# Maxima of the feature map in PSUM, constants on GpSimd, omega's parts read from PSUM, and half of one expert's second low parts on VectorE

## The chip, the cores and the metric

The program runs on one core of one Trainium2 chip. A core has TensorE for matrix products, VectorE and ScalarE for element work (both reach SBUF and PSUM), GpSimd for element work in SBUF, and DMA queues. The metric is the device time of one execution in microseconds; lower is better.

## The reference

Three layers follow each other. The first is an attention by random features: queries and keys of 2 batches, 8 heads, 576 tokens and 64 dimensions are projected on 128 features, and kv sums take the place of a matrix of scores:

```python
def phi(x):
    proj = np.einsum('bhsd,md->bhsm', x, omega)
    h = proj - np.sum(x * x, axis=-1, keepdims=True) / 2.0
    h = h - np.max(h, axis=-1, keepdims=True)
    return np.exp(h) / np.sqrt(m)
q_p, k_p = (phi(q_s), phi(k_s))           # q and k scaled
kv = np.einsum('bhsm,bhsd->bhmd', k_p, v)
z = np.sum(k_p, axis=2)
out = einsum(q_p, kv) / (einsum(q_p, z) + 1e-06)
```

The 1152 tokens of 512 values go on to a layer of 8 experts (512 to 1024 to 512, ReLU between), of which each token takes the one with the largest gate logit, weighted by its softmax value and by a sigmoid of a second gate. The third layer has 4 experts of the same size; every token runs through all of them, weighted by given probabilities. All is in float32.

## The kernel before

Products that need float32 accuracy are made of three passes of a faster format: every operand is kept as a high part `hi` (a rounding copy on ScalarE) and a low part `lo = src - hi` (VectorE or GpSimd), and `mm3` adds hi x hi, hi x lo and lo x hi. `split` (L88 to L90) makes both parts.

**The attention stage** takes the time until about 113 us. Its unit is a bank: four blocks of 128 tokens by 128 features, one PSUM bank. There are 36 banks in a fixed list `banks`: for each batch `b` and half of the heads `hh`, four banks of keys and four of queries, and, with batch 0, one bank each of the remaining 64 tokens of both batches ("rest"). Loop L513 walks over the list; at step `st` it does, in program order,

- `squares` (L211) for a group that begins: the sums of x * x, on VectorE for the very first group (a product L220 and a reduction L221 for four blocks at a time, four pairs), else on GpSimd (L223, and L227 six times, halving); loads of a later group; at step 12 `prep_late` (L190), which makes constants that the gates need;
- `stage_a` (L231): four transposes into PSUM, ScalarE's scaled high part qTh (L241), VectorE's low part qTl (L242), both read from that PSUM tile;
- `stage_b` (L247) for the bank one step back: six projection matmuls with omega's parts omh and oml (L259 to L261), VectorE's maximum over the features (L263), two VectorE steps on 128 x 4 elements that join it with the squares (L267 to mx, L268 to nb), four exponentials on ScalarE with nb as bias (L275);
- `do_c` for the bank four steps back: for keys the kv matmuls (L289) into the PSUM tile kv and, with a group's last, ScalarE's copy of it to SBUF (L311); for queries transposes of e (L320) and their copy (L323, L325);
- `do_d` for the bank six steps back: the products with kvs (L337), their division (L340 to L343), transposes back, and the parts xh and xl (L357, L358); after a batch its `gate`.

The instructions are written in this order; a scheduler fixes each engine's own queue ahead of the run, and keeps the order of any two accesses that it takes to conflict. PSUM has eight banks, all given out: two for transposes (`ps_t`), three for projections (`ps_j`), two for products (`ps_n`), one for kv (`ps_k`, of which a kv sum takes 260 of 512 columns). The maxima lie in SBUF:

```python
mx = ap.tile([128, 2, 2], F32, tag="mx", name="mx", bufs=4)
nc.vector.tensor_reduce(mx, ps, axis=AX.X, op=ALU.max)
STT(mx, s, -hs, mx, op0=ALU.mult, op1=ALU.add)
STT(nb, s, -hs, mx, op0=ALU.mult, op1=ALU.subtract)
```

**Omega** comes over ScalarE's queue, is transposed into PSUM (L180), copied to an SBUF tile omT that holds zeros elsewhere (L182), and split from there: omh on ScalarE (L185), oml on VectorE (L186).

**The gates.** `gate` computes the logits (L371), evacuated in two pieces by ScalarE (L372) and VectorE (L373), and picks for each batch the expert with most tokens; `gate_math` and `gate_count` do the rest (L410 to L455, cnt). E0 is batch 0's expert; its first weights are loaded with low parts on GpSimd (`load1`), its second ones by `load2`, eight pieces with low parts on GpSimd too (L90). `unit1` and `unit2` run one expert over one of four chunks of 288 tokens; `unit2` first makes a row of gate values (L585 on TensorE, from VectorE's L582 and L583). The tokens of other experts go through a loop over (expert, chunk) pairs that `extras` lists on VectorE; their sums go into x2T, whose chunks 2 and 3 GpSimd clears ahead (L683).

**The last layer** is a pipeline with seven products in place of eight for 2 x 2 blocks, and takes the rest of the time. The diff does not touch it.

## Time and profile before

| what | value |
|---|---|
| median of 3 runs | 641.92 us (639.6 to 644.51) |
| the profiled execution | 640.9 us |
| its span, first to last instruction | 638.5 us |
| TensorE busy | 614.5 us, 96% |
| TensorE's weight loads busy | 564.1 us, 88% |
| VectorE busy | 437.9 us, 69% |
| ScalarE busy | 263.2 us, 41% |
| GpSimd busy | 265.3 us, 42% |
| granted TensorE clock, mean | 0.997 of full |

PE is TensorE, PEld its weight loads, DVE VectorE, ACT ScalarE, POOL GpSimd. Shares of the whole span hide that the stages have different limits; the stretches of the first 134 us are to be read by themselves. A float32 matmul of kv or of the division leaves two records, one of the projections one. An instruction that waits for a port inside its execution shows as a long one, not as idle time.

### The profile page before, as it was taken

Reading aid. Unit: us, or ns where it says so; the run is one execution under the profiler, and the core shown is the slowest. Engines: PE = TensorE matmul, PEld = TensorE weight load, DVE = VectorE, ACT = ScalarE, POOL = GpSimd, SP = SyncE. Lnnn points to the kernel's source line nnn. Section 1 sums busy time; section 2 is a strip of 40 time slices with the busy share of each in tenths; the row PEclk is TensorE's granted clock in tenths of the full one; section 3 lists DMA queues with packets and bytes.
Section 4 is the critical chain, followed back from the end, with each engine's and each line's share of the span. In section 5 each row is a group of like instructions: output and inputs, shape, how many; then the busy total and the mean of one; then the engine's idle time right before and its main releaser. Section 6 shows DMA issues by size and latency. Waiting matters only on the chain.

```text
span 638.5 us, 10737 instructions
## 1 busy us (share of the span) xinstructions
PE 614.5 (96%) x3985; PEld 564.1 (88%) x3986; DVE 437.9 (69%) x947; ACT 263.2 (41%) x630; POOL 265.3 (42%) x303
## 2 busy tenths in 40 slices
PE   7899999989998999899999999999999999999997
PEld 6788898889998999689989899899899898898995
DVE  6898588885284568976766756756666667666564
ACT  4658575504062234534434433433433343343230
POOL 3994024700000001557537536646646645745220
PEclk9999999989999999999999999999999999999999
DMA  8621034005133302201201201102201102100004
GB/s 200 154 67 34 2 133 132 2 4 195 67 131 133 132 2 67 66 2 37 97 1 59 73 1 67 68 0 67 67 1 66 67 1 67 66 1 2 0 1 148
DMA packets 38180, 39.60 MB, mean 62 GB/s; under 512 B 14448, under 2 KB 26736, under 8 KB 38128
## 3 DMA queue, kind: packets, MB, share of 16 engines
q1 hardware_dynamic: 37840, 38.85, 19.5%
q8 instruction: 31, 0.51, 0.3%
q14 instruction: 21, 0.17, 0.1%
q10 hardware_dynamic: 288, 0.07, 0.0%
HBM read 36.55 MB, written 2.36 MB: 61 GB/s over the span
## 4 chain that ended last, share of the span: by engine, by line
PE 84%; DVE 8%; POOL 3%; issue 1%; SPq 1%; DMA 1%; ACT 1%; POOLq 0%; ACTq 0%
PE po L553 10%; PE po L552 10%; PE po L554 10%; PE pp L552 9%; PE pp L554 9%; PE pp L553 9%; PE py L552 3%; PE py L554 3%; PE py L553 3%; PE ph L553 3%; PE ph L552 3%; PE ph L554 3%; PE pnd L337 2%; POOL x L227 2%; PE kv L289 2%
## 5 line engine op out<-in xcount | busy, mean ns | idle before, releaser
L90 POOL TENSOR_TENSOR wlo<-st,whi 128x512 fp32r<-128x512 f32 x104 | 126.4, 1238 | 241.5 <-ACT whi L89 241.5
L89 ACT CAST whi<-st 128x512 fp32r<-128x512 f32 x144 | 81.8, 596 | 141.4 <-PE po L554 51.9
L874 DVE SCALAR_TENSOR_TENSOR oacc<-po,pb,oacc 128x512 f32<-128x512 f32 x135 | 100.1, 749 | 56.0 <-PE po L554 56.0
L554 PE MATMUL po<-whi,hl 128*128 128x512 f32 x288 | 112.1, 390 | 0.7 <-POOL hl L548 0.6
L552 PE MATMUL po<-whi,hh 128*128 128x512 f32 x288 | 112.5, 391 | 0.0
L553 PE MATMUL po<-wlo,hh 128*128 128x512 f32 x288 | 112.4, 390 | 0.0
L548 POOL TENSOR_TENSOR hl<-c,hh 128x320 fp32r<-128x320 f32 (+1 forms) x64 | 53.2, 831 | 89.1 <-ACT hh L547 76.5
L552 PE MATMUL pp<-xh,whi 128*128 128x320 f32 (+1 forms) x256 | 75.8, 297 | 0.4 <-DVE u L833 0.2
L554 PE MATMUL pp<-xh,wlo 128*128 128x320 f32 (+1 forms) x256 | 75.7, 296 | 0.0
L553 PE MATMUL pp<-xl,whi 128*128 128x320 f32 (+1 forms) x256 | 75.7, 296 | 0.0
L554 PEld LDWEIGHTS po<-whi,hl 128*128 128x128 f32 x288 | 54.0, 188 | 12.9 <-POOL hl L548 1.0
L552 PEld LDWEIGHTS po<-whi,hh 128*128 128x128 f32 x288 | 54.1, 188 | 10.6 <-ACT hh L542 0.2
L553 PEld LDWEIGHTS po<-wlo,hh 128*128 128x128 f32 x288 | 54.1, 188 | 10.0
L821 DVE TENSOR_TENSOR c<-u,pp 128x320 f32<-128x320 f32 (+1 forms) x96 | 43.2, 453 | 21.7 <-PE pp L554 21.2
L546 ACT ACTIVATE c<-c 128x320 f32<-128x320 f32 (+1 forms) x64 | 28.5, 445 | 54.4 <-DVE c L821 53.7
L552 PEld LDWEIGHTS pp<-xh,whi 128*128 128x128 f32 x256 | 48.4, 190 | 2.3 <-DVE u L839 0.6
L553 PEld LDWEIGHTS pp<-xl,whi 128*128 128x128 f32 x256 | 48.5, 190 | 1.2
L552 PE MATMUL ph<-xh,whi 128*128 128x288 f32 (+1 forms) x160 | 47.9, 299 | 1.7 <-issue 1.7
L552 PE MATMUL py<-hh,whi 128*128 128x288 f32 x160 | 49.1, 307 | 0.0
L554 PEld LDWEIGHTS pp<-xh,wlo 128*128 128x128 f32 x256 | 48.5, 190 | 0.0
L553 PE MATMUL ph<-xl,whi 128*128 128x288 f32 (+1 forms) x160 | 48.0, 300 | 0.0
L543 DVE SCALAR_TENSOR_TENSOR hl<-c,hh 128x320 fp32r<-128x320 f32 (+1 forms) x64 | 45.9, 751 | 3.0 <-ACT hh L542 3.0
(217 smaller groups left out, 1424.5 us busy)
## 6 DMA issues: line engine op xcount, KB each, us to landing
st<-in_moe_w_dram SPq DMA_DIRECT2D x32, 512.0 KB, 4.1
st<-in_moe_w_dram SPq DMA_DIRECT2D x12, 1024.0 KB, 5.4
v<-in_v_dram SPq DMA_DIRECT2D x16, 128.0 KB, 3.9
q<-in_q_dram SPq DMA_DIRECT2D x4, 512.0 KB, 5.2
out_dram<-oacc SPq DMA_DIRECT2D x8, 256.0 KB, 2.1
k<-in_k_dram SPq DMA_DIRECT2D x3, 512.0 KB, 5.1
k<-in_k_dram SPq DMA_DIRECT2D x4, 128.0 KB, 2.7
kr<-in_k_dram SPq DMA_DIRECT2D x2, 128.0 KB, 3.6
```

The costliest lines, as they stand in the source:

```text
L89: nc.scalar.copy(hi, src)
L90: eng.tensor_tensor(lo, src, f32(hi), op=ALU.subtract)
L227: nc.gpsimd.tensor_tensor(dst, x2[:, :, 0:w], x2[:, :, w:2 * w], op=ALU.add)
L289: nc.tensor.matmul(kvps[key][:, i, :], e[i][r0:r1], v65[i], start=first and i == 0, stop=last and i == G - 1)
L543: STT(hl, src, 0.0, f32(hh), op0=ALU.max, op1=ALU.subtract)
L546: nc.scalar.activation(c, c, AF.Relu)
L548: nc.gpsimd.tensor_tensor(hl, c, f32(hh), op=ALU.subtract)
L552: nc.tensor.matmul(ps, sh_, mh, start=start, stop=False)
L553: nc.tensor.matmul(ps, sh_, ml, start=False, stop=False)
L554: nc.tensor.matmul(ps, sl_, mh, start=False, stop=stop)
L821: TT(c, u, p, op=op)
L874: STT(oacc[:, T], po, pc, oacc[:, T], op0=ALU.mult, op1=ALU.add)
```

## The change

1. The maxima mx are put into the upper 32 columns of the kv bank, eight places of four columns in turn (`MXS`). The bank is now one tile kbank for the whole stage, of which the kv sums take the first 260 columns. L267 reads and writes mx there, L268 reads it.
2. omT goes. omh and oml are cleared by VectorE, and both parts are made from the transposed PSUM tile, for 64 partitions at a time. In the first group's squares the third and fourth pair are queued behind the last of these.
3. For the first tile of keys the copies qTh and qTl come in two halves.
4. Constants: fold, iota, iota1, rev, ue, uc and the clearing of lgr go from VectorE to GpSimd, ahead of all squares (`prep_first`); cmask stays in `prep_late`. Of the rest of `prep_late`, the low part of the gate weights, one addition and the product pb go to GpSimd, while a reduction and the reciprocal between them stay on VectorE.
5. `load2` takes a list of engines; E0's low parts alternate between VectorE and GpSimd.
6. The clearing of x2T's chunks 2 and 3 is written behind `extras` and the second `unit1`.

`load_rest` gets a parameter for its queue, with the queue of before as default.

```diff
-        def load2(self):
+        def load2(self, engs=None):
...
-                    self.part(w2p, "w2", self.w2, [128, DM], st[:, j, :])
+                    self.part(w2p, "w2", self.w2, [128, DM], st[:, j, :], engs[j % len(engs)] if engs else None)
...
+    nc.vector.memset(f32(omh), 0.0)
+    nc.vector.memset(f32(oml), 0.0)
...
     for r in range(2):
-        nc.scalar.copy(omT[64 * r:64 * r + 64, r, :], pt[64 * r:64 * r + 64, 0, :])
...
-    nc.scalar.copy(omh, omT)
-    TT(oml, omT, f32(omh), op=ALU.subtract)
+        rows = slice(64 * r, 64 * r + 64)
+        nc.scalar.copy(omh[rows, r, :], pt[rows, 0, :])
+        om_done = TT(oml[rows, r, :], pt[rows, 0, :], f32(omh[rows, r, :]), op=ALU.subtract)
...
+    GT, GS, GC = nc.gpsimd.tensor_tensor, nc.gpsimd.tensor_scalar, nc.gpsimd.tensor_copy
+
+    def prep_first():
+        GT(fold, ident[:, 0:32], ident[:, 32:64], op=ALU.add)
+        GT(fold, fold, ident[:, 64:96], op=ALU.add)
+        GT(fold, fold, ident[:, 96:128], op=ALU.add)
+        nc.gpsimd.iota(i32, pattern=[[1, 32]], base=0, channel_multiplier=0)
+        GC(iota, i32)
+        GS(iota1, iota, 1.0, None, op0=ALU.add)
+        GS(rev, iota[:, 0:NE], -1.0, float(NE), op0=ALU.mult, op1=ALU.add)
+        GC(ue, iota[:, 0:NE].unsqueeze(1).to_broadcast([128, 4, NE]))
+        GC(uc, iota[:, 0:4].unsqueeze(2).to_broadcast([128, 4, NE]))
+        nc.gpsimd.memset(lgr, 0.0)
...
-        split(wgh, wgl, wg)
+        split(wgh, wgl, wg, nc.gpsimd)
...
-        TS(ds_, ds_, 1e-9, None, op0=ALU.add)
+        GS(ds_, ds_, 1e-9, None, op0=ALU.add)
         nc.vector.reciprocal(ds_, ds_)
-        TT(pb, dpr, ds_.unsqueeze(2).to_broadcast([128, 9, NE2]), op=ALU.mult)
-
+        GT(pb, dpr, ds_.unsqueeze(2).to_broadcast([128, 9, NE2]), op=ALU.mult)
...
+        if first:
             for h in range(0, n, 4):
-                TT(x2[:, h:h + 4], x[:, h:h + 4], x[:, h:h + 4], op=ALU.mult)
-                nc.vector.tensor_reduce(s[:, h:h + 4], x2[:, h:h + 4], axis=AX.X, op=ALU.add)
+                with tc.issue_after(om_done.ins) if h >= 8 else nullcontext():
+                    TT(x2[:, h:h + 4], x[:, h:h + 4], x[:, h:h + 4], op=ALU.mult)
+                    nc.vector.tensor_reduce(s[:, h:h + 4], x2[:, h:h + 4], axis=AX.X, op=ALU.add)
...
-        nc.scalar.activation(t[:, :n], ps[:, :n], AF.Copy, scale=SCALE)
-        STT(tl[:, :n], ps[:, :n], SCALE, f32(t[:, :n]), op0=ALU.mult, op1=ALU.subtract)
+        step = 2 if (kind, b, hh) == ("k", 0, 0) else n
+        for i in range(0, n, step):
+            part = slice(i, i + step)
+            nc.scalar.activation(t[:, part], ps[:, part], AF.Copy, scale=SCALE)
+            STT(tl[:, part], ps[:, part], SCALE, f32(t[:, part]), op0=ALU.mult, op1=ALU.subtract)
...
+    kbank = ps_k.tile([128, 512], F32, tag="kv", name="kv")
...
-        mx = ap.tile([128, 2, 2], F32, tag="mx", name="mx", bufs=4)
+        m0 = 512 - 4 * MXS + 4 * (flip[0] % MXS)
+        mx = kbank[:, m0:m0 + 4].rearrange("p (a c) -> p a c", a=2)
...
-            kvps[b, hh] = ps_k.tile([M, G, D + 1], F32, tag="kv", name="kv")
+            kvps[b, hh] = kbank[:, 0:G * (D + 1)].rearrange("p (g d) -> p g d", g=G)
...
-    E0.load2()
+    E0.load2((nc.vector, nc.gpsimd))
     unit2(0, E0.w2, hs)
+    nx_t, mt, le_t, lc_t = extras()
+    hs = unit1(1, E0.w1)
     for c in (2, 3):
         for cols in x2cols(c):
             nc.gpsimd.memset(x2T[:, :, cols], 0.0)
-    nx_t, mt, le_t, lc_t = extras()
-    hs = unit1(1, E0.w1)
```

## Rows read from the trace of the kernel before

**Rows 1.** Busy time of each engine by stretch (instructions), granted clock, DMA share.
```profile
20.00:60.00 40.00, 35.69 (x276) 31.48 (x274) 37.76 (x91) 25.99 (x86) 33.50 (x52) 1.00 0.33 81
60.00:90.00 30.00, 29.93 (x253) 27.49 (x252) 21.47 (x82) 19.16 (x61) 0.00 (x0) 1.00 0.14 48
...
120.00:127.00 7.00, 6.43 (x48) 6.19 (x49) 6.76 (x13) 2.15 (x6) 7.00 (x7) 1.00 0.00 0
127.00:130.50 3.50, 1.59 (x13) 1.29 (x11) 3.36 (x26) 0.41 (x1) 0.00 (x1) 0.99 0.00 0
130.50:134.00 3.50, 3.46 (x13) 3.17 (x14) 3.23 (x21) 0.40 (x1) 0.00 (x0) 0.52 0.00 0
```

**Rows 2.** VectorE's groups, 14 to 57 us: line, operation, count, busy, mean ns, idle.
```profile
L267 DVE SCALAR_TENSOR_TENSOR mx<-sq,mx 128x4 f32<-128x4 f32 x16 | 9.4, 586 | 0.1
L268 DVE SCALAR_TENSOR_TENSOR nb<-sq,mx 128x4 f32<-128x4 f32 x16 | 7.0, 438 | 0.2
...
L207 DVE TENSOR_TENSOR pb<-dpr,ds__528 128x36 f32<-128x36 f32 x1 | 1.8, 1825 | 0.0
...
L358 DVE TENSOR_TENSOR xl<-pnd,xh 128x256 fp32r<-128x256 f32 x4 | 1.7, 417 | 0.3 <-ACT xh L357 0.2
```

**Rows 3.** The same two groups, 57 to 91 us.
```profile
L267 DVE SCALAR_TENSOR_TENSOR mx<-sq,mx 128x4 f32<-128x4 f32 x13 | 2.0, 156 | 0.1
L268 DVE SCALAR_TENSOR_TENSOR nb<-sq,mx 128x4 f32<-128x4 f32 x13 | 2.0, 154 | 0.0
```

**Rows 4.** Timeline, VectorE and GpSimd: start, us, engine, line, what, [idle before].
```profile
14.42 1.89 POOL L223 TENSOR_TENSOR x<-q 128x1024 f32<-128x1024 f32 x1 [3.29 <-DMA q<-in_q_dram]
...
15.18 1.15 DVE L267 SCALAR_TENSOR_TENSOR mx<-sq,mx 128x4 f32<-128x4 f32 x1
...
19.81 0.22 POOL L227 TENSOR_TENSOR sq<-x 128x16 f32<-128x16 f32 x1
...
21.20 0.64 DVE L267 SCALAR_TENSOR_TENSOR mx<-sq,mx 128x4 f32<-128x4 f32 x1
...
28.99 0.22 POOL L227 TENSOR_TENSOR sq<-x 128x16 f32<-128x16 f32 x1
...
33.23 0.15 DVE L267 SCALAR_TENSOR_TENSOR mx<-sq,mx 128x4 f32<-128x4 f32 x1
```

**Rows 5.** Timeline around the two gates, 80 to 131 us.
```profile
80.73 0.19 DVE L392 TENSOR_TENSOR gm_eq<-lg,gm_mx 128x40 f32<-128x40 f32 x1
...
120.67 1.26 DVE L392 TENSOR_TENSOR gm_eq<-lg,gm_mx 128x40 f32<-128x40 f32 x1
...
124.47 2.53 POOL L90 TENSOR_TENSOR wlo<-st,whi 128x512 fp32r<-128x512 f32 x2
...
125.73 1.30 DVE L400 SCALAR_TENSOR_TENSOR cb<-cs,cbm,rev 128x8 f32<-128x8 f32 x1
...
130.54 1.32 PE L585 MATMUL pg<-dg,ones 128*128 128x288 f32 x2 [1.41 <-DVE cnt L455]
```

**Rows 6.** Timeline of the start, GpSimd, VectorE and the weight loads.
```profile
7.07 1.19 POOL L223 TENSOR_TENSOR x<-kr 128x512 f32<-128x512 f32 x1 [5.55 <-DMA kr<-in_k_dram]
...
7.23 1.06 DVE L199 COPY ue<-iota 128x32 f32<-128x32 f32 x1
...
8.76 0.19 PEld L260 LDWEIGHTS pj<-oml,qTh 128*128 128x128 f32 x1 [2.22 <-DVE oml L186]
```

**Rows 7.** Line L373 by itself: durations in ns, and its engine's idle time.
```profile
L373 DVE COPY lgr<-lgp x4: 179/180/861, 76.1 to 118.7; 16x32 f32<-16x32 f32 x4
...
  ACT lgs L372: 2.4, 3
```

**Rows 8.** Timeline of TensorE, a full kv batch.
```profile
45.94 2.00 PE L289 MATMUL kv<-v,e 128*128 128x65 f32 x16
```

**Rows 9.** Line L90 by itself, on both engines: min/median/max ns.
```profile
L90 POOL TENSOR_TENSOR wlo<-st,whi x104: 737/1294/2050, 91.9 to 594.3; 128x512 fp32r<-128x512 f32 x90, 128x256 fp32r<-128x256 f32 x14
...
L90 DVE TENSOR_TENSOR wlo<-st,whi x40: 424/686/694, 147.9 to 241.0; 128x512 fp32r<-128x512 f32 x38, 128x256 fp32r<-128x256 f32 x2
```

More of the change, by code (lines that the diff above doesn't have):

```diff
@@ L1 @@
 from collections import deque
-from contextlib import ExitStack
+from contextlib import ExitStack, nullcontext
 import concourse.bass as bass
@@ L33 @@
 EB, FLIP = 6, 1
+MXS = 8
 SCALE = 1.0 / (D ** 0.25)
@@ L113, in load2, with part @@
                 for j in range(4):
-                    self.part(w2p, "w2", self.w2, [128, DM], st[:, j, :])
-        def part(self, pool, tag, sink, shape, src):
+                    self.part(w2p, "w2", self.w2, [128, DM], st[:, j, :], engs[j % len(engs)] if engs else None)
+        def part(self, pool, tag, sink, shape, src, eng=None):
             hi = pool.tile(shape, F32R, tag=tag + "h", name="whi")
             lo = pool.tile(shape, F32R, tag=tag + "l", name="wlo")
-            split(hi, lo, src, self.eng)
+            split(hi, lo, src, eng or self.eng)
             sink.append((hi, lo))
@@ L140, in load_main, with load_rest @@
         return t
-    def load_rest(src, tag, width=D):
+    def load_rest(src, tag, width=D, q=nc.sync):
         t = ap.tile([128, H, width], F32, tag=tag, name=tag, bufs=1)
         for b in range(2):
-            nc.sync.dma_start(t[64 * b:64 * b + 64, :, 0:D], src[b, :, 512:576, :].rearrange("h p d -> p h d"))
+            q.dma_start(t[64 * b:64 * b + 64, :, 0:D], src[b, :, 512:576, :].rearrange("h p d -> p h d"))
         if width > D:
@@ L174, in moe_stack @@
         nc.sync.dma_start(dpr[64 * b:64 * b + 64, 8, :], dprobs[S * b + 512:S * b + 576])
-    omT = cp.tile([128, 2, M], F32, name="omT")
-    nc.vector.memset(omT, 0.0)
+    omh = cp.tile([128, 2, M], F32R, name="omh")
+    oml = cp.tile([128, 2, M], F32R, name="oml")
+    nc.vector.memset(f32(omh), 0.0)
+    nc.vector.memset(f32(oml), 0.0)
     pt = ps_t.tile([128, 4, 128], F32, tag="pt", name="pt")
@@ L181, in moe_stack @@
     for r in range(2):
-        nc.scalar.copy(omT[64 * r:64 * r + 64, r, :], pt[64 * r:64 * r + 64, 0, :])
-    omh = cp.tile([128, 2, M], F32R, name="omh")
-    oml = cp.tile([128, 2, M], F32R, name="oml")
-    nc.scalar.copy(omh, omT)
-    TT(oml, omT, f32(omh), op=ALU.subtract)
+        rows = slice(64 * r, 64 * r + 64)
+        nc.scalar.copy(omh[rows, r, :], pt[rows, 0, :])
+        om_done = TT(oml[rows, r, :], pt[rows, 0, :], f32(omh[rows, r, :]), op=ALU.subtract)
     wgh = cp.tile([128, KB, 16], F32R, name="wgh")
@@ L199, in prep_late @@
-        nc.vector.tensor_copy(ue, iota[:, 0:NE].unsqueeze(1).to_broadcast([128, 4, NE]))
-        nc.vector.tensor_copy(uc, iota[:, 0:4].unsqueeze(2).to_broadcast([128, 4, NE]))
-        nc.vector.memset(lgr, 0.0)
-        split(wgh, wgl, wg)
+        split(wgh, wgl, wg, nc.gpsimd)
         ds_ = cp.tile([128, 9], F32, name="ds_")
         nc.vector.tensor_reduce(ds_, dpr, axis=AX.X, op=ALU.add)
-        TS(ds_, ds_, 1e-9, None, op0=ALU.add)
+        GS(ds_, ds_, 1e-9, None, op0=ALU.add)
         nc.vector.reciprocal(ds_, ds_)
-        TT(pb, dpr, ds_.unsqueeze(2).to_broadcast([128, 9, NE2]), op=ALU.mult)
+        GT(pb, dpr, ds_.unsqueeze(2).to_broadcast([128, 9, NE2]), op=ALU.mult)
@@ L209, in moe_stack, with squares @@
+    prep_first()
     sq, st_a, st_e = {}, {}, {}
-    def squares(kind, b, hh, eng):
+    def squares(kind, b, hh, first=False):
         src = raw[kind, b, hh] if b < 2 else raw[kind, 2]
@@ L217, in squares @@
         s = ap.tile([128, n], F32, tag="sq" + kind + ("r" if b == 2 else ""), name="sq")
[L218 removed]
+        if first:
             for h in range(0, n, 4):
[L220 to L221 removed]
+                with tc.issue_after(om_done.ins) if h >= 8 else nullcontext():
+                    TT(x2[:, h:h + 4], x[:, h:h + 4], x[:, h:h + 4], op=ALU.mult)
+                    nc.vector.tensor_reduce(s[:, h:h + 4], x2[:, h:h + 4], axis=AX.X, op=ALU.add)
         else:
[L223 removed]
+            GT(x2, x, x, op=ALU.mult)
             w = D // 2
@@ L226, in squares @@
                 dst = x2[:, :, 0:w] if w > 1 else s.unsqueeze(2)
-                nc.gpsimd.tensor_tensor(dst, x2[:, :, 0:w], x2[:, :, w:2 * w], op=ALU.add)
+                GT(dst, x2[:, :, 0:w], x2[:, :, w:2 * w], op=ALU.add)
                 w //= 2
@@ L240, in stage_a @@
             nc.tensor.transpose(ps[:, i, :], blk.rearrange("p a d -> p (a d)"), ident)
-        nc.scalar.activation(t[:, :n], ps[:, :n], AF.Copy, scale=SCALE)
-        STT(tl[:, :n], ps[:, :n], SCALE, f32(t[:, :n]), op0=ALU.mult, op1=ALU.subtract)
+        step = 2 if (kind, b, hh) == ("k", 0, 0) else n
[3 more added lines that the diff above has]
+            STT(tl[:, part], ps[:, part], SCALE, f32(t[:, part]), op0=ALU.mult, op1=ALU.subtract)
         st_a[kind, b, hh, jp] = t, tl
+    kbank = ps_k.tile([128, 512], F32, tag="kv", name="kv")
+    kvps = {}
     flip = [0]
@@ L283, in heads @@
         return [st_e[kind, b, hh, j // 2, i // 2][:, i % 2, j % 2, :] for i in range(G)]
-    kvps, kvs = {}, {}
+    kvs = {}
     def kv_part(key, e, v65, first, last, r0, r1):
@@ L516, in moe_stack @@
             if b < 2 and jp == 0 and hp == 0:
-                squares(kind, b, hh, nc.vector if (kind, b, hh) == ("k", 0, 0) else nc.gpsimd)
+                squares(kind, b, hh, (kind, b, hh) == ("k", 0, 0))
                 if kind == "k" and (b, hh) != (0, 0):
@@ L522, in moe_stack @@
             if b == 2 and hh == 0:
-                squares(kind, 2, 0, nc.gpsimd)
+                squares(kind, 2, 0)
             if st == LATE:
```

9 lines of the change are left out of this document (removed).

## The prediction

> **What bounds the kernel now.** I read the 40 slices of the page first, then the stretches of the first 134 us, the groups of VectorE, the timeline of VectorE and GpSimd, and the waits. After 134 us TensorE runs with few gaps, and the diff touches nothing there but the time of two memsets, so what it can do lies ahead of that point. In the slices the reader is to see that VectorE is fullest where GpSimd is busy with squares. The stretches say it in numbers [rows 1]: from 20 to 60 us VectorE is busy 37.76 of 40 us and TensorE has 276 matmul records, 6.9 per us; from 60 to 90 us, with GpSimd idle, VectorE falls to 21.47 of 30 us and TensorE has 253 records, 8.4 per us. At the second pace the 276 would take 32.7 us: 7.3 us go to something other than TensorE's own work.
>
> The groups show to what. With GpSimd busy, from 14 to 57 us, the two VectorE steps on four elements, L267 and L268, take 586 and 438 ns on the mean [rows 2]; with it idle, from 57 to 91 us, 156 and 154 ns [rows 3]. That is 16 x 0.430 + 16 x 0.284 = 11.4 us of waiting inside instructions. The timeline shows for what [rows 4]: an L267 starts at 15.18 while a square runs on GpSimd from 14.42 for 1.89 us, and ends at 16.33, with that square. L358 holds 417 ns under the same squares [rows 2]: it reads one operand from PSUM and one from SBUF, where L267 and L268 read both from SBUF.
>
> The second place is the gate of batch 1. From 120.67 us five small VectorE steps take 1.26, 1.30, 1.33, 0.70 and 1.30 us (the first and the last stand in the rows), where the first of them took 0.19 for batch 0 with GpSimd idle [rows 5]: about 4.9 us too long together, beside GpSimd's low parts of the first expert's second weights, which last until 127.0. TensorE pays a little later [rows 1]: it idles 0.57 us in 120 to 127 and 1.91 us in 127 to 130.5, mostly for the reduction of the counts [rows 5], and behind that idle stretch its granted clock is 0.52, the lower of the two levels (1.2 GHz), for 3.5 us: 3.5 x 0.48 = 1.7 us of lost work. Together 4.2 us.
>
> **The change, part by part**, against the profiled execution: 640.9 us, of which the span is 638.5 and 2.4 lie around it. The median of the runs, 641.92, is 1.0 us above it.
>
> (a) Omega's parts straight from PSUM, ahead of the later squares; constants to GpSimd at the start. Now the low part L186 is queued behind four pairs of squares and eight constants, one of which, L199, took 1.06 us beside a square of GpSimd, and TensorE's weight load waits 2.22 us for it [rows 6]. The change takes the constants and the later two pairs of squares from in front of it, so the first maxima can come up to 2.2 us earlier. On GpSimd the ten constants, at about the 0.22 us of its smallest step [rows 4], make 2.2 us and fall into its idle 5.55 us ahead of 7.07 [rows 6]; if one meets a square of VectorE, that square waits 0.2 us, and this chain has 2 us more than before. But the next squares wait for the DMA of the queries until 14.42 [rows 4], which is issued as before, so only what TensorE and VectorE finish ahead of that counts. The copies of the first tile in two halves lengthen its chain by about a handover and hide in the same wait. Between 0 and 2.0 us; I take 1.0, since half of the time until 14.42 is DMA wait for both engines.
>
> (b) Maxima in PSUM. L267 and L268 then read one SBUF operand each; by L358 they keep their 0.15 us under squares. VectorE gains the 11.4 us, and 1.6 more as L207, 1.83 us for 36 elements [rows 2], goes to GpSimd. TensorE can take no more of it than its 7.3 us, and not all of that where GpSimd sets the pace, at 5.6 us for a group of squares (14.42 to 20.03): the squares of the first queries end at 20.03 and the L267 that needs them starts at 21.20; the squares of the second keys end at 29.21 and their L267 is at 33.23 [rows 4]. So the point at 33 us can come at most 4.0 us earlier; behind it the squares' lead grows and the rest can follow. Between 3.0 us (a point short of that) and 7.3; I take three quarters of the slack, 5.5. What prep_late now puts on GpSimd (a low part of 64 elements, two steps under 40) is some 0.8 us and lies in that lead. Its reciprocal on VectorE now waits for a GpSimd step that stands behind squares, and behind the reciprocal wait the next maxima and low parts, once, for up to one square, 1.89 us; inside the lower end.
>
> (c) The price of (b): the maxima lie in the PSUM bank of the kv sums. The nearest case in the trace is L372 and L373, where ScalarE and VectorE read different columns of one PSUM tile [rows 7]: no data goes from one to the other, yet VectorE waited for ScalarE in three of four cases, 2.4 us. So two engines' accesses to one PSUM tile are kept in program order, and each kv batch on TensorE will wait for the maxima of its own step, the next maxima for the batch, and both for ScalarE's evacuation. A full batch is 16 records, 2.00 us [rows 8]; there are eight, and four half ones for the rest rows. Serial throughout, VectorE would stand 8 x 2.0 + 4 x 1.0 = 20 us, and behind its waiting reduction stand the low parts qTl and xl and the copy qpT, for which TensorE waits next. Below nothing it can't go, since no instruction gets shorter by the order. Against the far end: a batch comes in every second step at most, VectorE has 8.5 us to spare in 30 [rows 1], and TensorE has transposes and projections of the next bank to put in front. I take 12 batches at 0.2 us, a handover as between ScalarE and VectorE at L373 and not the batch itself: 2.4 us, with 0 and 20 kept.
>
> (d) Half of the first expert's second low parts on VectorE. GpSimd loses 4 x 1.294 = 5.2 us, VectorE gets 4 x 0.686 = 2.7 us [rows 9], each with two SBUF operands, so each may also wait for one of GpSimd's four, and the gate's steps stand behind them in VectorE's queue. The high parts come from 115 us on; taken in turns, both halves end near 121 us instead of 127.0 [rows 5]. The two memsets of about 1 us each now come after the lists, and may still meet the gate's steps. Of the 4.9 us some 3 should go, and with them most of TensorE's 2.5 us and part of its clock loss: between 0 (the low parts on VectorE cost what they free) and 4.2; I take 3.0. The Trainium skill, page "SBUF — State Buffer", section "Who interferes with whom", says that a VectorE step with two SBUF inputs contends with a GpSimd instruction that reads SBUF and not with one that only writes it. By that rule the memsets would not hold up the gate, the term would be 4.2 and the time 1.2 us lower; no row here shows a memset beside such a step.
>
> Sum: 1.0 + 5.5 - 2.4 + 3.0 = 7.1 us, 633.8 in the profiled execution and **634.8** by the median.
>
> **Rivals**, by the median too.
> 1. TensorE binds anyway. It is already busy 35.69 of 40 us from 20 to 60 [rows 1]; if VectorE's waits only fill time that other handovers (exponentials, the lag between the steps) would take, (b) gives no more than (c) costs, and (d) half: 641.9 - 1.0 - 1.5 = 639.4. For it: busy TensorE; against it: VectorE at 94% in the same stretch.
> 2. The bank ties TensorE to VectorE, and the kernel gets slower. Place: the kv batches between 15 and 97 us. Price: serial in two thirds of the cases, 13 us, against 6 us left of (a) and (b) and 2 of (d): 641.9 + 5 = 647. It decides from a price of 9 us, 0.75 us a batch. For it: rows 7, and that the order of each queue is fixed ahead, so a wait at its head stops all behind it. The Trainium skill, page "PSUM — Partial Sum Buffer", section "PSUM bank collisions raise a hardware error", has the rule that PSUM is to be guarded by bank and quadrant, not by address; this rival is what that rule brings here, and rows 7 are the trace's case of it.
> 3. The moved operand does not free the steps, as the other is still in SBUF, and the change doesn't do what it says. Of (b) only L207's 1.6 us stays: 641.9 - 1.0 - 1.6 + 2.4 - 3.0 = 638.7. Against it: L358 [rows 2].
>
> **How the numbers follow.** Chances: forecast 0.58, rival 1 0.21, rival 2 0.14, rival 3 0.07. The low end has every term at its best and no price: 2.0 + 7.3 + 4.2 = 13.5, 628. The high end is rival 2 up to a price of 11 us, 645, which leaves out about half of it. About 1%, 6.4 us, is what a measurement of this kernel can tell from no change: below 635.5 is faster, above 648.3 slower. Three quarters of the forecast's chance lie below the first bound, 0.43, since its range goes down to 628 and up only to where rival 1 begins; the rest of it, rivals 1 and 3 and 0.03 of rival 2 are the same, 0.46; slower is 0.11.
>
> **What would show it.** (a): the weight load of oml without its 2.22 us, the queries' squares still at 14.4. (b): L267 and L268 near 0.15 us from 14 to 57 us, TensorE's records from 20 to 60 us near 8 per us. (c): idle time ahead of kv matmuls put down to L268, or ahead of the maxima put down to kv; some us of either is rival 2. (d): the low parts over by about 121 us, the counts reduced before 128 us, no stretch at the low clock behind. What would make it wrong: the added dependences arrange each engine's queue anew, and waits may arise where no row of before shows any.

## The result: 0.5% slower, where 1.1% faster was forecast

| | before | after |
|---|---|---|
| median of 20 runs each | 641.09 us (638.43 to 645.59) | 645.3 us (641.78 to 647.45) |
| the profiled execution | 640.9 us | 642.2 us |
| its span, mean granted clock | 638.5 us, 0.997 | 640.4 us, 0.992 |

The ratio is 1.0054, with an interval of 1.0034 to 1.0073: slower, by less than the 1% that the prediction took as the least that can be told from no change. The time is 10.5 us above the forecast and 0.3 us above the range's upper end. The 20 executions after lie in two groups, nine from 641.78 to 643.05 us with a mean clock of 0.991 to 0.995, and eleven from 644.71 to 647.45 us with 0.982 to 0.989. The profiled one is of the lower group, so its trace shows only part of what the median lost. Slow executions, more than 1.5% above the fastest of their kernel, are left out of all medians and ratios below (one each in E3, E12 and E17, two each in E16 and E18).

**What the forecast wanted of VectorE is there.** The stretches of after, in the columns of [rows 1]:

```profile
10.00:20.00 10.00, 7.55 (x53) 6.70 (x52) 5.99 (x18) 7.00 (x24) 6.42 (x12) 0.90 1.07 237
20.00:60.00 40.00, 36.17 (x270) 33.35 (x270) 24.24 (x77) 22.37 (x71) 33.65 (x54) 0.91 0.30 80
60.00:90.00 30.00, 29.29 (x242) 26.44 (x241) 21.54 (x84) 18.74 (x62) 0.05 (x1) 1.00 0.08 23
...
127.00:130.50 3.50, 3.37 (x26) 3.40 (x27) 3.25 (x23) 1.06 (x3) 0.00 (x0) 1.00 0.02 5
130.50:134.00 3.50, 3.50 (x30) 3.50 (x30) 2.21 (x14) 0.82 (x2) 0.00 (x0) 1.00 0.00 0
```

From 20 to 60 us VectorE is busy 24.24 us, against 37.76 in [rows 1]: 13.5 us less. VectorE's groups from 14 to 57 us, as [rows 2] (the line numbers have moved by 14):

```profile
L277 DVE TENSOR_REDUCE kv<-pj 128x4 f32<-128x512 f32 x16 | 11.1, 697 | 8.5 <-PE kv L303 8.0 <-PE pj L274 0.2
...
L281 DVE SCALAR_TENSOR_TENSOR kv<-sq,kv 128x4 f32<-128x4 f32 x16 | 2.6, 160 | 0.2
L282 DVE SCALAR_TENSOR_TENSOR nb<-sq,kv 128x4 f32<-128x4 f32 x16 | 2.4, 150 | 0.3
```

The two small steps take 160 and 150 ns under squares, where they took 586 and 438. But TensorE has 270 records in that stretch, no more than the 276 of before, and its granted clock is 0.91 there instead of 1.00.

**Where VectorE's free time went.** Its first row above says it: 8.0 us of idle time ahead of the maxima, ended by kv matmuls. Three of the waits of the first 130 us (engine, line, waited for: us in total, times, longest), the maxima's, one of TensorE's weight loads for projections, and the late chain's:

```profile
DVE kv L277 <- PE kv L303: 10.3, 6, 2.7
...
PEld pj L272 <- ACT e L289: 4.8, 6, 1.9
...
DVE ds__521 L211 <- POOL ds__521 L210: 3.2, 1, 3.2
```

The timeline shows both kinds of VectorE's waits (start, us, engine, line, what, idle time before):

```profile
19.16 1.90 PE L303 MATMUL kv<-v,e 128*128 128x65 f32 x16
...
21.09 0.70 DVE L277 TENSOR_REDUCE kv<-pj 128x4 f32<-128x512 f32 x1 [2.70 <-PE kv L303]
...
23.83 1.89 PE L303 MATMUL kv<-v,e 128*128 128x65 f32 x16
...
25.76 0.70 DVE L277 TENSOR_REDUCE kv<-pj 128x4 f32<-128x512 f32 x1 [2.26 <-PE kv L303]
...
32.14 1.96 POOL L234 TENSOR_TENSOR x<-x 128x256 f32<-128x256 f32 x4
...
34.48 0.26 POOL L210 TENSOR_SCALAR ds__521<-ds__521 128x9 f32<-128x9 f32 x1
34.77 0.22 DVE L211 RECIPROCAL ds__521<-ds__521 128x9 f32<-128x9 f32 x1 [3.23 <-POOL ds__521 L210]
34.90 0.10 DVE L282 SCALAR_TENSOR_TENSOR nb<-sq,kv 128x4 f32<-128x4 f32 x1
35.04 1.14 ACT L289 ACTIVATE e<-pj,nb 128x128 f32<-128x128 f32 x4 [2.76 <-DVE nb L282]
...
35.46 0.33 PE L334 MATMUL pt<-ident,e 128*128 128x128 f32 x1 [2.37 <-ACT e L289]
```

A maximum starts when a whole kv batch is over: 21.09 is 0.03 us after the end of the batch from 19.16, 25.76 is 0.04 after the end of the one from 23.83. And at 34.77 the reciprocal of `prep_late` has waited 3.23 us for GpSimd's addition, which stood behind the folds of a group's squares; behind it wait nb, the exponentials for nb, and TensorE for the exponentials, 2.37 us. Behind this gap the granted clock is lower (TensorE in the first two columns, the clock third from the end):

```profile
26.00:28.00 2.00, 2.00 (x12) 1.98 (x10) 1.41 (x4) 1.25 (x5) 1.76 (x4) 0.50 0.32 72
...
30.00:36.00 6.00, 3.63 (x34) 3.49 (x32) 2.68 (x8) 2.30 (x7) 5.26 (x12) 0.99 0.61 182
36.00:38.00 2.00, 2.00 (x11) 2.00 (x11) 1.80 (x6) 0.78 (x4) 1.92 (x2) 0.50 0.00 0
38.00:40.00 2.00, 2.00 (x14) 2.00 (x13) 1.88 (x10) 1.77 (x7) 1.76 (x4) 0.68 0.00 0
```

TensorE is busy 3.63 us of the 6 from 30 to 36 us, and then works at the lower level, 1.2 GHz, for some 3.3 of the next 4 us by the two clocks: 2 x 0.50 + 2 x 0.32 = 1.6 us of work lost. Not every gap is followed so: from 12 to 14 us TensorE is busy 0.50 of 2 us, and the clock stays at 1.00 up to 24 us.

**The start and the gate** look in part as the prediction wanted them. Omega's low part and the first maximum, and GpSimd's squares of the queries; the last row is the first maximum of before:

```profile
5.97 0.29 DVE L187 TENSOR_TENSOR oml<-pt,omh 64x128 fp32r<-64x128 f32 x1 [0.33 <-ACT omh L186]
...
9.21 0.70 DVE L277 TENSOR_REDUCE kv<-pj 128x4 f32<-128x512 f32 x1 [0.17 <-PE pj L274]
...
13.89 1.89 POOL L230 TENSOR_TENSOR x<-q 128x1024 f32<-128x1024 f32 x1 [2.87 <-DMA q<-in_q_dram]
```
```profile
10.14 1.29 DVE L263 TENSOR_REDUCE mx<-pj 128x4 f32<-128x512 f32 x2 [0.23 <-PE pj L261]
```

The first maximum starts at 9.21 instead of 10.14 us, while the squares of the queries still wait for their DMA. The gate of batch 1, against [rows 5], and under it two rows of before:

```profile
118.32 2.15 POOL L699 MEMSET x2T<- 128x1024 f32 x3 [13.04 <-PE pnd L360]
...
121.86 5.06 POOL L91 TENSOR_TENSOR wlo<-st,whi 128x512 fp32r<-128x512 f32 x3
...
124.78 0.24 DVE L395 COPY lg<-lgt 128x80 f32<-128x80 f32 x1 [0.59 <-PE lgt L393]
...
125.94 1.05 DVE L406 TENSOR_TENSOR gm_eq<-lg,gm_mx 128x40 f32<-128x40 f32 x1
127.99 0.23 DVE L414 SCALAR_TENSOR_TENSOR cb<-cs,cbm,rev 128x8 f32<-128x8 f32 x1
...
137.92 0.52 DVE L619 TENSOR_TENSOR x2T<-py,gb 128x256 f32<-128x256 f32 x2
```
```profile
120.17 0.24 DVE L381 COPY lg<-lgt 128x80 f32<-128x80 f32 x1 [0.21 <-PE lgt L379]
...
135.71 0.52 DVE L605 TENSOR_TENSOR x2T<-py,gb 128x256 f32<-128x256 f32 x2 [1.01 <-PE py L554]
```

cb takes 0.23 us (1.30 before), and the clock stays at 1.00 from 130.5 to 134 us (0.52 before). From the logits to the first expert's first output 13.1 us pass; before, 15.5 (120.17 to 135.71). The gate comes 4.6 us late, though, at 124.78: in this execution all that is lost is lost ahead of it. And the low parts are not over by about 121 us but at 126.92. Though the memsets are now written later, GpSimd still runs most of them first, from 118.32 to 120.47, ahead of its low parts.

### The profile page after: what moved, and what is told of

Read it like the earlier page. It is cut to its first block, busy times and chain, and to the rows that moved or that the text cites. A ratio compares the mean times of both kernels' runs of the same rounds, so it can differ in the third digit from the quotient of the medians.

```text
span 640.4 us, 10753 instructions
## 1 busy us (share of the span) xinstructions
PE 617.0 (96%) x3985; PEld 567.0 (89%) x3986; DVE 423.0 (66%) x943; ACT 263.1 (41%) x631; POOL 263.2 (41%) x311
## 4 chain that ended last, share of the span: by engine, by line
PE 86%; POOL 4%; DVE 4%; ACT 2%; issue 2%; SPq 1%; DMA 1%; POOLq 0%; ACTq 0%
PE po L568 10%; PE po L567 10%; PE po L566 10%; PE pp L566 9%; PE pp L568 9%; PE pp L567 9%; PE py L566 3%; PE ph L568 3%; PE py L568 3%; PE ph L566 3%; PE py L567 3%; PE ph L567 3%; PE kv L303 2%; PE pnd L351 2%; POOL x L234 2%
## 5 line engine op out<-in xcount | busy, mean ns | idle before, releaser
L91 POOL TENSOR_TENSOR wlo<-st,whi 128x512 fp32r<-128x512 f32 x100 | 122.3, 1244 | 240.3 <-ACT whi L90 240.3
L90 ACT CAST whi<-st 128x512 fp32r<-128x512 f32 x144 | 82.0, 597 | 138.2 <-PE po L568 52.0
L568 PE MATMUL ph<-xh,wlo 128*128 128x288 f32 (+1 forms) x160 | 48.0, 300 | 0.0
```

What stands on the lines that cost most here:

```text
L90: nc.scalar.copy(hi, src)
L91: eng.tensor_tensor(lo, src, f32(hi), op=ALU.subtract)
L568: nc.tensor.matmul(ps, sl_, mh, start=False, stop=stop)
```

## The experiments

Medians are given, and the ratio to before from runs on the same chip, with its interval; runs on different chips are best compared by their ratios; before's own median was 641.64 beside E1 to E4, 641.17 beside E5 to E8, 640.18 beside E9 to E12, 639.6 beside E13 to E15 and 641.04 beside E16 to E18.

### The parts of the change undone, and alone

**E1: the changed kernel, maxima back in SBUF.**

```diff
-        mx = kbank[:, m0:m0 + 4].rearrange("p (a c) -> p a c", a=2)
+        mx = ap.tile([128, 2, 2], F32, tag="mx", name="mx", bufs=4)
```

> The changed kernel with the maxima back in SBUF and kv in a tile of its own. Theory 1 (the shared bank: the maxima wait for kv batches, 10.3 us in the changed kernel's trace, and TensorE's gaps there drop its clock): the waits of the maxima on kv fall to 0, the small steps are long again under squares, and the time is 638 to 641, 4 us or more below the changed kernel's 645.3. Theory 2 (the split late chain: VectorE's reciprocal stood 3.2 us for a GpSimd step, TensorE idled 2.4 us behind it and ran at the lower clock for some 3 us): that stall stays, 644 to 646.

640.61 us, 0.9986 (0.9961 to 1.0011). Putting the maxima back, port waits and all, makes the changed kernel 4.7 us faster (4.4 by the two ratios). The reciprocal's wait is still there, but shorter:

```profile
DVE ds__532 L211 <- POOL ds__532 L210: 1.4, 1, 1.4
```

**E2: the changed kernel, late chain back on VectorE.**

```diff
-        GS(ds_, ds_, 1e-9, None, op0=ALU.add)
+        TS(ds_, ds_, 1e-9, None, op0=ALU.add)
         nc.vector.reciprocal(ds_, ds_)
-        GT(pb, dpr, ds_.unsqueeze(2).to_broadcast([128, 9, NE2]), op=ALU.mult)
+        TT(pb, dpr, ds_.unsqueeze(2).to_broadcast([128, 9, NE2]), op=ALU.mult)
```

> The changed kernel with the addition and the product of the late chain back on VectorE, so that its reciprocal waits for no GpSimd step. Theory 2: the 3.2 us wait ahead of the reciprocal and the low clock from 36 to 39.5 us are gone, 640 to 642. Theory 1: that stall goes, but the kv waits (10 us) and the low clock behind them stay, 643 to 645.

642.33 us, 1.0002 (0.9977 to 1.0027), between what the two theories expected: 3.0 us of the loss go with these two instructions, and so does the upper group of executions (641.53 to 643.72 in 12 runs). TensorE's records stand in the same order as in the changed kernel. The maxima wait for kv as there, 11.3 us. The low part of the gate weights stays on GpSimd, here and in E1, E5, E13 and E14.

**E3: before, with the maxima in the kv bank and nothing else.**

> The kernel before with nothing but the maxima in the kv bank. As forecast (5.5 us gained, 2.4 paid): 638. Theory 1: the price is as large as the gain or larger, 641 to 645, with the small steps near 0.15 us and some 10 us of waits of the maxima on kv. Theory 2: the loss is the late chain's alone, 637 to 639.

642.44 us, 0.9981 (0.9948 to 1.0013): no difference that can be told. 6.5 us of waits of maxima for kv stand against the 11.4 us of port waits.

**E4: before, with the second low parts in turns and the later memsets alone.**

```diff
-    E0.load2()
+    E0.load2((nc.vector, nc.gpsimd))
```

> The kernel before with nothing but half of the first expert's second low parts on VectorE and the memsets written later. As forecast for that term: 3.0 us gained, 638, and no stretch at the lower clock near 131 us. Rival: VectorE pays for the low parts what it saves in waits, 641, with the lower clock still behind the gate.

641.69 us, 0.9996 (0.9968 to 1.0025). The gate does what the prediction wanted, 12.5 us from the logits to the first output (123.88 to 136.41), 3.0 less than before, but the time doesn't follow. Its timeline around the gate, two stretches, and the first of them in before:

```profile
117.23 0.68 DVE L90 TENSOR_TENSOR wlo<-st,whi 128x512 fp32r<-128x512 f32 x1
...
117.54 1.03 POOL L685 MEMSET x2T<- 128x1024 f32 x1
...
123.88 0.24 DVE L381 COPY lg<-lgt 128x80 f32<-128x80 f32 x1 [0.36 <-PE lgt L379]
...
124.13 1.73 POOL L90 TENSOR_TENSOR wlo<-st,whi 128x512 fp32r<-128x512 f32 x1 [0.61 <-ACT whi L89]
...
125.82 0.19 DVE L392 TENSOR_TENSOR gm_eq<-lg,gm_mx 128x40 f32<-128x40 f32 x1
...
136.41 0.51 DVE L605 TENSOR_TENSOR x2T<-py,gb 128x256 f32<-128x256 f32 x2
```
```profile
10.00:20.00 10.00, 8.59 (x59) 7.81 (x60) 7.44 (x18) 5.85 (x22) 6.51 (x11) 0.83 1.11 242
...
120.00:127.00 7.00, 5.37 (x28) 4.68 (x26) 5.61 (x14) 2.62 (x8) 5.25 (x3) 0.76 0.01 4
```
```profile
10.00:20.00 10.00, 8.86 (x72) 8.23 (x72) 7.06 (x18) 6.62 (x23) 6.00 (x12) 1.00 0.99 235
```

TensorE's order is that of before (two of its 3985 records stand elsewhere, behind the logits), yet this execution reaches the logits at 123.88 us, 3.7 us later than the one of before, with a clock of 0.83 from 10 to 20 us where that had 1.00. One execution is no measure of 3 us in this stage, here and wherever two traces are set beside each other. The stretch at the lower clock has not gone but come earlier: 7 x 0.24 = 1.7 us of work from 120 to 127 us, as much as before lost from 130.5 to 134.

**E5: the start and the second low parts, without the maxima in PSUM and without the late chain.** (E1's and E2's edits together.)

> The changed kernel with the maxima in SBUF again and the late chain (the addition and the product pb) on VectorE again: omega's parts, the early constants and the second low parts are left of the change. If the two parts undone in E1 and E2 alone carry the loss, both undone leave the gain of the second low parts and some of the start: 638 to 640 us, ratio to before 0.995 to 0.998, and the lm spread of the runs narrow. If the losses are of the clock, which falls after some idle stretch or other whatever the order, no difference can be seen: 641 to 642.5. In the trace: no wait of a maximum on kv, small steps on four elements at about 0.5 us under squares as before.

640.84 us, 0.9992 (0.9967 to 1.0017): 0.3 us below before where the prediction's terms (a) and (d) make 4.0. Against E1 the late chain costs nothing here.

### The port waits and the shared bank, each by itself

**E9: before, squares left out, both small steps kept.** The steps read zeros.

```diff
-            s = sq[kind, b, hh].rearrange(...)
+            s = zs.rearrange(...)
...
-                squares(kind, b, hh, nc.vector if (kind, b, hh) == ("k", 0, 0) else nc.gpsimd)
```

> The kernel before with the squares left out (they cancel) and both steps on four elements kept, which read zeros in their place and the maxima in SBUF: the port waits are gone and nothing else is changed on VectorE. This is my term (b) by itself, forecast at 3.0 to 7.3 us. With a quarter of a microsecond of work gone per step, some 636 us if the term was of the right size; within 1 us of 630.5 (the time with the steps gone altogether) if the port waits were all; 640 or more if the waits were not what held TensorE and the gain of the negated maxima came from the two instructions less in the chain from maximum to exponential. Small steps at 0.15 us throughout.

635.51 us, 0.9919 (0.9889 to 0.995), 4.7 us faster. The stretch from 20 to 60 us and VectorE's groups from 14 to 57:

```profile
20.00:60.00 40.00, 38.90 (x319) 36.13 (x318) 31.23 (x105) 28.69 (x95) 0.25 (x2) 1.00 0.31 81
```
```profile
L265 DVE TENSOR_REDUCE mx<-pj 128x4 f32<-128x512 f32 x19 | 13.0, 684 | 10.5 <-PE pj L263 10.4
...
L270 DVE SCALAR_TENSOR_TENSOR nb<-zs,mx 128x4 f32<-128x4 f32 x18 | 2.7, 152 | 0.1
L269 DVE SCALAR_TENSOR_TENSOR mx<-zs,mx 128x4 f32<-128x4 f32 x18 | 2.6, 149 | 0.0
```

TensorE has 319 records, 8.0 per us, and the maxima wait for projections, not for kv. Over the whole run its records stand in the same order as in before. The port waits did hold TensorE, by about as much as the prediction said. (The first group's four pairs of squares on VectorE are gone too, so this is rather the upper side of the term.)

**E10: E9 with the maxima in the kv bank.**

> As the run before in this list, and the maxima in the upper columns of the kv bank, as in the changed kernel. No port wait is left that the move could take away, so what it costs is the tie alone: by my theory 4 to 8 us slower than with the maxima in SBUF, with some 10 us of maxima waiting for kv. By the prediction's term (c) 2.4 us. By the rival that other waits of the order take its place anyway, under 1 us.

642.17 us, 1.001 (0.9987 to 1.0033): **this edit alone costs 6.7 us** (5.8 by the two ratios). Two of its waits in the first 130 us and the stretch from 20 to 60 us:

```profile
PEld pj L264 <- ACT e L281: 6.2, 10, 1.1
...
DVE kv L269 <- PE kv L295: 7.5, 5, 2.3
```
```profile
20.00:60.00 40.00, 37.57 (x301) 33.76 (x300) 29.07 (x95) 26.57 (x87) 0.25 (x2) 1.00 0.30 80
```

TensorE falls from 319 to 301 records at the same clock: 18 records, 2.3 us at 8 per us, in this stretch alone.

The edit does two things at once. The maxima wait for kv, and the ties make the scheduler fix another order: 436 of TensorE's 3985 records stand elsewhere than in E9. TensorE itself pays ahead of projections, which wait for exponentials that still read an earlier bank: 6.2 us here, 5.5 in E3, 4.8 in the change, and no such wait in E9. Three of the ten waits here, at 10.59, 11.89 and 15.96 us, come ahead of the first maximum that waited for kv (23.17), so they belong to the new order and not to a batch. How much of the 6.7 us is order and how much the waits for batches was not told apart.

**E11 and E12: a bank of their own for the maxima, squares kept; and its control.** The projections give up one of three banks for it; E12 takes the bank away and does nothing else.

```diff
-    ps_j = ctx.enter_context(tc.tile_pool(name="ps_j", bufs=3, space=PSUM))
+    ps_j = ctx.enter_context(tc.tile_pool(name="ps_j", bufs=2, space=PSUM))
+    ps_m = ctx.enter_context(tc.tile_pool(name="ps_m", bufs=1, space=PSUM))
```

> The kernel before with the maxima in a PSUM bank of their own, for which the projections give one of their three banks up; to be read against the run with two projection banks alone. The port waits are gone and no kv batch shares the bank. If the tie is what the change lost by, this is 3 to 6 us faster than the run with two projection banks and shows no wait of a maximum on kv; if the port waits don't hold TensorE, the two are alike.

> The kernel before with two banks for the projections in place of three and nothing else: the control for the run with a bank of its own. The last layer uses the same ring, so some microseconds slower than before are possible: 641 to 650 us.

E11 645.25 us, 1.0071 (1.0042 to 1.01); E12 650.62 us, 1.0176 (1.0131 to 1.022). With squares running and without the tie, maxima in PSUM gain 5.4 us (6.7 by the ratios); with the tie (E3) they gained nothing. No maximum waits for kv in E11:

```profile
DVE mb L267 <- PE pj L264: 12.7, 16, 1.7
```

Here too the order is new, with 468 records elsewhere than in E12, and this one did no such harm. The lost projection bank costs 10 us, so this is no way out.

**E6 and E7: the maximum negated by its own reduction.** A row's half sum of squares is subtracted from every feature and again with their maximum, so it cancels; E6 still computes the squares and doesn't use them, E7 leaves them out.

```diff
-        nc.vector.tensor_reduce(mx, ps, axis=AX.X, op=ALU.max)
...
-        STT(mx, s, -hs, mx, op0=ALU.mult, op1=ALU.add)
-        STT(nb, s, -hs, mx, op0=ALU.mult, op1=ALU.subtract)
+        nc.vector.tensor_reduce(nb, ps, axis=AX.X, op=ALU.max, negate=True)
```

> The kernel before, in which the bias of the exponentials is written by the reduction itself as the negated maximum: a row's half sum of squares is subtracted from every feature and again from their maximum, so it cancels. The squares are still computed on GpSimd but not used. This takes the port waits away (no step on four elements is left) without any tie to the kv bank. If VectorE's 11.4 us of port waits were a limit of TensorE and the bank took the gain away (my theory), TensorE gains 4 to 6 us: 635.5 to 638, with 6 to 8 us more slack of VectorE between 20 and 60 us and some 290 TensorE records there. If TensorE is bound by its own work, by handovers and by its clock (rival 1 of the prediction), VectorE becomes emptier and the time stays: 640 to 642.

> As the run with the negated maxima, and the squares, which nothing uses, are left out: GpSimd is idle to about 100 us and so is its share of the port. If what is left of the wait under squares (one low part in SBUF, copies with an SBUF operand) costs anything, 1 to 2 us below the run with the squares kept; if not, the same time within 1 us. By the rival, that TensorE binds, also 640 to 642.

631.21 us, 0.9834 (0.9798 to 0.987), and 630.47 us, 0.9826 (0.979 to 0.9862): 10 us, twice what I expected. Whether GpSimd computes squares makes no difference that can be told, with no small step left that reads two SBUF operands. By the ratios E7 is 6.0 us below E9, which differs by 72 steps of 0.15 us, 10.8 us of VectorE's time and of the way from a maximum to its exponentials; which of the two counts was not told apart.

### The small terms and the order of the queues

**E14: the start alone on before. E15: the late chain alone on before.**

```diff
-        split(wgh, wgl, wg)
+        split(wgh, wgl, wg, nc.gpsimd)
...
-        TS(ds_, ds_, 1e-9, None, op0=ALU.add)
+        nc.gpsimd.tensor_scalar(ds_, ds_, 1e-9, None, op0=ALU.add)
```

(E15's edit, with the product pb on GpSimd too; E14's is omega, the split copies and the early constants of the change, and the first line above, the gate weights' low part on GpSimd.)

> The kernel before with the start of the change alone: omega's parts straight from PSUM ahead of the later squares, the first copies in two halves, the early constants on GpSimd. By the prediction's term (a) 1.0 us faster; by the sum of the start and the second low parts together (0.3 us faster in an earlier run, the second low parts alone 0.3) nothing, within 0.7 us of before.

> The kernel before with the late chain alone split over both engines: the gate weights' low part, the addition and the product on GpSimd, the sum and the reciprocal on VectorE. If the chain costs by itself what undoing it gave in the changed kernel, 3 us slower, 644; if it costs only where the maxima are tied to the kv bank (undone beside maxima in SBUF it gave nothing), within 0.7 us of before, with a wait of the reciprocal of under 2 us.

E14 643.13 us, 1.0056 (1.0032 to 1.008); E15 646.14 us, 1.0109 (1.0065 to 1.0152): 3.5 and 6.5 us slower, both against what I expected. E14's runs had a median clock of 0.986 against 0.993 of before's, which at 430 us for a whole unit (last section) would be 3.0 of its 3.5 us. That is rough: its run with the lowest clock, 0.942, took 643.51 us, and one at 0.986 took 643.39. E15's reciprocal waits 1.9 us, once; that can't be 6.5 us. But its three moved instructions shifted much else: in the order of their starts, 168 of TensorE's 3985 records and some 90 of VectorE's 947 stand elsewhere than in before. (In the same way 154 of TensorE's do in E16 and 39 in E17; the expectations below count lines of a listing, more for the same moves.)

**E16: before, `prep_late` written at step 14 in place of 12. E17: at step 13. E18: E15 at step 14.** No instruction of E16 and E17 is other than in before; only the order is.

```diff
-LATE = 12
+LATE = 14
```

> The kernel before with the block of late constants written at step 14 in place of 12: not one instruction is added, removed or given to another engine, but 455 lines of TensorE's queue stand elsewhere, nearly as in the run with the late chain alone (60 lines from that one's). If the order of the queues made that run 6.5 us slower, this one is 644 to 647 as well; if it was the reciprocal's wait for GpSimd, which doesn't exist here, 639 to 641, as before.

> As the run before in this list with step 13: 84 lines of TensorE's queue and 66 of VectorE's stand elsewhere than before. If the fixed order alone moves the time by microseconds, this differs from before by an amount that nothing in the edit tells, 0 to 4 us either way; if order doesn't matter, within 0.7 us.

> The late chain split over GpSimd and VectorE, written at step 14: 42 lines of TensorE's queue from the run with the whole chain on VectorE at step 14, so the difference of the two is the split at nearly the same order. If the split costs by itself, 2 to 6 us slower than that run; if the order was all, within 1 us of it.

E16 644.3 us, 1.0066 (1.0032 to 1.01); E17 642.75 us, 1.002 (0.9997 to 1.0043); E18 642.85 us, 1.001 (0.9975 to 1.0044). **E16's order alone costs 3.3 us** (4.2 by the ratio); E17's 1.7 us are within its interval. The stretch from 20 to 60 us of E16, at a clock of 1.00, in the fastest of its executions:

```profile
20.00:60.00 40.00, 33.88 (x262) 29.91 (x261) 36.97 (x88) 24.74 (x80) 32.56 (x51) 1.00 0.31 81
```

262 records against 276 [rows 1], with VectorE as full as before. At that order the split chain costs nothing (E18 is 1.5 us below E16, within the intervals). E15's order is nearly E16's (16 of TensorE's records apart), so half or more of E15's 6.5 us goes with its order; the rest is open, since E18 has the same split and doesn't lose it. Part of E16's loss comes with the clock: on the mean of the runs it was 0.989 in E16 and 0.992 in before, which at 430 us for a whole unit (last section) is 1.4 of the 3.3 us; whether the order brings the lower clock, by other gaps, or chance did, was not told apart. TensorE's queue of E16 against that of before, a piece of the difference (+ is E16; line, what, times in a row):

```
 L260 MATMUL pj<-oml,qTh 128x256
+L261 MATMUL pj<-omh,qTl 128x256
+L259 MATMUL pj<-omh,qTh 128x256
+L260 MATMUL pj<-oml,qTh 128x256
+L261 MATMUL pj<-omh,qTl 128x256
 L289 MATMUL kv<-v_148,e 128x65 x5
```

Here a bank's projections go ahead of a kv batch that they stood behind; which of such moves costs is not settled.

### Versions that beat both kernels

**E8: E7 with the second low parts in turns. E13: the changed kernel without its maxima in PSUM, negated, without squares.**

> The negated maxima, no squares, and of the change only the second low parts in turns on VectorE and GpSimd with the later memsets. If the terms add, 1.5 to 2.5 us below the run without squares: 633 to 636 us. If the clock takes back what idle TensorE time gives (as after the second low parts alone, 641.7 at a lower clock), within 1 us of the run without squares.

> The changed kernel without its maxima in PSUM, with the maximum negated by its reduction and the squares left out, since they cancel; omega's parts, the constants, the late chain and the second low parts stay as in the change. With the ties and the port gone, the start and the second low parts may show what they are worth: 627 to 630 us if they add their 1 to 3 us to the negated maxima alone; 630 to 631.5, as without them, if TensorE is by now bound by itself up to the gate.

E8 630.43 us, 0.9833 (0.9798 to 0.9868); E13 632.69 us, 0.9886 (0.9866 to 0.9906). E6, E7 and E8 are alike and 10 to 11 us faster than before. E13, with most of the rest of the change, gains 7 us, less than expected and less than they do; the rest of the change adds nothing to the negated maxima. E7 is the simplest.

## Why the prediction was wrong, by its own steps

Sizes by the medians of the runs above, gains positive:

| term | forecast | measured | by |
|---|---|---|---|
| (b) port waits gone | 5.5 (3.0 to 7.3) | 4.7 | E9 against before |
| (c) price of the bank | -2.4 (0 to -20) | -6.7 | E10 against E9 |
| (a) and (d) together | 1.0 + 3.0 | 0.3 | E5 against before |
| late chain split | inside (b)'s lower end | -3.0 | E2 against after |
| sum | 7.1 | -4.7 | measured whole: -4.2 |

The sum fits better than it should, which is luck: the terms depend on each other, as E14 and E15 show, and E10 and E5 also have an order of their own (436 and 282 records elsewhere), where E9 and E2 have that of the kernel they stand against.

**(c) is the step that failed most**, by 4.3 of some 11 us; (a) and (d) together failed by 3.7 and the late chain by 3.0. (c) saw the place, the direction and the far end, and took "12 batches at 0.2 us, a handover as between ScalarE and VectorE at L373 and not the batch itself". For VectorE it was the batch itself: the five or six waits that are left are up to 2.7 us long. The 0.2 us was not in the row either: [rows 7] has 2.4 us in three waits, 0.8 each, and 12 of those make 9.6 us. The reason given against the far end, that VectorE has time to spare and TensorE has other work to put in front, did not hold: the order is fixed, and what was put in front, the projections, waited for exponentials (6.2 us in E10) more than for the low parts that (c) named (0.9 us for qTl, 1.0 for xl). And only the maxima wait: no kv batch waits for a maximum in E3, E10 or the change. Rival 2 has that reason, and the result, 645.3, lies nearest to it (647), but by another sum: its price was not reached, 6.7 us where it decides from 9, and the kernel is slower because (a) and (d) gave 0.3 us in place of 4.0 and the late chain took 3.0. The chance of 0.11 for a slower kernel doesn't follow from rival 2 either, as its own 647 lies below the 648.3 from which the prediction calls it slower. The Trainium skill, page "PSUM — Partial Sum Buffer", section "PSUM bank collisions raise a hardware error", has the rule that PSUM is to be guarded by bank and quadrant, not by address. E10's 7.5 us of maxima waiting for kv, with no data going between them, agree with it. An access without such an order was not tried.

**(b) was right**, in its mechanism (160 and 150 ns under squares) and, by E9 (4.7 us) and by E11 against E12 (5.4), in its size. Rivals 1 and 3 are out: TensorE took up the freed time in E9, with 319 records where it had 276.

**(d) was right from the logits to the first output** (2.4 us less in the change, 3.0 in E4) **and not in the time of E4.** Of E4's missing gain a part lies beside a lower clock, 0.988 on the mean of its runs against 0.991 of before's: at 430 us for a whole unit of clock (below) 1.3 us. The rest is within E4's interval, which reaches down to 0.9968. E5 differs from E14 by (d) alone and is 4.1 us faster by the two ratios, on different chips and with a median clock of 0.9895 against 0.986. What (d) is worth by itself stays open. E4's rows agree with the rule that the prediction weighed, from the Trainium skill, page "SBUF — State Buffer", section "Who interferes with whom"; the time that it would have given, 1.2 us lower, still didn't come. VectorE's low part from 117.23 us and GpSimd's memset from 117.54 ran side by side, and neither took longer than alone (0.68 us, its median being 0.686 [rows 9], and 1.03). GpSimd's low parts beside those of VectorE took 1.70 to 1.91 us, as at 124.13, and 1.30 alone. But a memset does not leave all of VectorE's steps alone. Two rows of before:

```profile
114.65 1.02 POOL L683 MEMSET x2T<- 128x1024 f32 x1 [9.98 <-ACT hh L542]
...
114.69 1.06 DVE L582 TENSOR_SCALAR dg<-ident,sel 128x128 f32<-128x128 f32 x1
```

L582, which multiplies one SBUF operand by a scalar, took 1.06 us beside the memset, where its median is 0.29, and the three steps behind it ended with it. L582 makes rows of gate values ahead of the logits, and the memsets meet it in the change too, at 118.32.

**(a)** moved the first maximum up by 0.9 us, and no gain was left: alone it made the kernel slower, beside a lower clock (E14), in company it gave next to nothing (E5, at 0.989 against 0.993: by that difference 1.5 us more at the same clock).

**The late chain** was priced at one square, 1.89 us. In the change the wait was 3.23 us, since the addition stood behind a whole run of folds, and the low clock behind the gap cost 1.6 more; undone, 3.0 us came back. But beside maxima in SBUF it costs nothing (E1 against E5), and on before 6.5 us, half or more of them with the order (E16). It has no price that holds at every order.

**What the prediction named and left out of its sum** is that an edit can have the scheduler fix the queues anew; its last sentence says so, and the range has nothing for it. The time of before is that of one order; of the two others that were tried, with not one instruction changed, one is 3.3 us slower, and one 1.7, which its interval does not tell from none. Terms of 1 to 3 us, worked out on the old order, were added as if it stayed.

## What to carry to other kernels

Before moving a small operand into a bank that another engine writes, price the ordering at that engine's whole batch, not at a handover, count in the new order of the queues that it brings, and test it by itself: the gain and its price were nearly equal here, and either alone would have been plain. Where a scheduler fixes the order of the queues, move one line without changing an instruction and time that first; what it moves (2 to 4 us here) is the least that a forecast of local terms can be sure to. And look for the instruction that needn't exist: removing two steps per bank gave more than twice what removing their waits gave.

## What the runs showed that was not expected

The granted clock differs from run to run of one kernel, and the time mostly goes with it: a straight line through the 120 executions of before that ran beside the experiments, at mean clocks from 0.978 to 0.999, gives 430 us for a whole unit, an estimate (for the 13 beside E13 to E15 alone it is 140). In the profiled executions most of the lower clock lies in the first 134 us; E4, whose TensorE order is that of before up to the logits, shows 0.83 between 10 and 20 us where before shows 1.00. Which gap brings it on in which execution was not found out.
